# Transposing p of ten tiles with VectorE and transfers instead of TensorE

## The chip, the cores and the metric

The kernel runs on one core of one Trainium2 chip, in one launch. The metric is the device time of that launch in microseconds (us). The program is built once and run several times; the median is given.

The engines are called as in the profile: PE is TensorE (matmuls; PEld are its weight loads), DVE is VectorE, ACT is ScalarE, POOL is GpSimd, SP is SyncE, which here issues nearly all DMAs. Each engine works through its own list of instructions in order, and waits for others by semaphores.

## What is computed

Two layers, each a Fourier mixing and then a mixture of 256 experts (PEER), on 2048 tokens of width 512, all in float32:

```python
def layer(x):
    xn = layernorm(x)
    a, b = xn @ dft_hid_re.T, xn @ dft_hid_im.T         # 512 x 512
    x = x + dft_seq_re @ a - dft_seq_im @ b             # 2048 x 2048
    xn = layernorm(x)
    q = einsum("nd,dhc->nhc", xn, w_q)                  # 32 heads, 2 x 128
    s1, s2 = q[..., :128] @ k1.T, q[..., 128:] @ k2.T   # 16 scores each
    # per head: the best 2 of s1 and of s2, their 4 sums, the best 2 of these
    g = softmax(top_s)                                  # over those 2
    act = gelu(einsum("nd,nhkd->nhk", xn, u[top_e]))
    return x + einsum("nhk,nhk,nhkd->nd", g, act, v[top_e])
```

The kernel doesn't gather rows of u and v. It computes gelu(xn @ u.T) for all 256 experts, multiplies it by a 2048 x 256 matrix of gates (the sum over heads of g at the experts that were picked), and calls the product p. The layer's output is then x + p @ v. Float32 accuracy comes from splitting each operand in a high part, rounded to what the matmul takes in one pass (float32r), and the low rest: high x high, high x low and low x high are three matmuls that add up in one PSUM bank.

## The kernel before, in words

**Tiles and units.** The 2048 tokens are 16 tiles of 128. The product with the sequence matrices, "seq", goes in units: seven units of 256 tokens (two tiles each) and two of 128 (one tile each), `ORDER` says in which order, and `at` is a unit's place in it, 0 to 8. In layer 0 the order is as numbered, so `at` 2 to 6 are tiles 4 to 13. A unit's seq is 16 steps over the tokens s, each of four matmul groups of three (L518), on pieces of the sequence matrix that are streamed: L454 loads a piece `raw` (four buffers), L458 makes its high part `ch` on ACT, L462 its low part `cl` on DVE (three buffers each).

**A token tile** (`token_tile`, L610) follows when its unit's seq is done. PE multiplies by the hidden matrices (L668), DVE adds the rows of x (L682) and takes the layernorm's statistics, ACT writes xn (L705). xn is transposed, multiplied by the folded query weights (L784, L788) and by u (L818). DVE then picks the experts (L880 to L1009), and the gates of the tile are built by small matmuls (L1057), copied (L1089), stored in DRAM (`gdr`, L1116) and loaded back as `gt` (L1124), one buffer. L1131 multiplies `act` by `gt`: that is p, 128 tokens x 256 experts, in the buffer `act` (three of them).

For the product with v, p has to be transposed, experts on the partitions. Before the change that is done like this in layer 0: `f_pt` (L1162) transposes p's two halves of 128 x 128 on PE into a PSUM bank, ACT copies the high part into `pp` (L1167), DVE makes the low part (L1170), six matmuls multiply by v's parts (L1181, L1185), DVE adds the result to the row (L1218), and the row is stored as `x2d` (L1228), from where layer 1 loads it (L1243).

**Two ways without PE are in the kernel already.** xn of layer 0's units from `at` 2 on (and of most of layer 1) is transposed by `turned` (L716): DVE transposes the 16 x 4 blocks of 32 x 32 each in its place (L722), SP stores the tile in DRAM (`xdr`, L726), and four DMAs (L735) read it back, one for each 32 rows, with the blocks in their new places; ACT and DVE then make the parts (L742, L745). And in layer 1 `deferred` tiles have p's blocks turned by DVE (L1138), split (L1142, L1145) and stored (L1153); their product with v is made at the end (`off`, L566).

**What sets the order.** The order of every engine's instructions is written out ahead, by a planner (`Plan`, L78). Each step is an `op` with an engine, an estimated time, what it comes after, which buffers it takes (`take`) and which it is the last user of (`last`), a priority, and for DMAs `lag`, the time from issue to landing, and `shy`, an extra allowance. The planner plays this through and sorts the steps by their planned start; seq steps fill PE's time between the steps of tiles. On the chip each engine then keeps to that order, also where a step is late. A change of one step's engine or time lets all later steps be ordered anew.

Of the kernel before, what the change touches and what calls it, by code (L numbers as in the profile page):

```python
# [8 lines left out]
F32 = mybir.dt.float32  # L9
# [7 lines left out]
P = 128  # L17
# [21 lines left out]

def MOVED(layer, at):  # L40
    return at >= 2 if layer == 0 else at < NCH + NSC * (TPC - 1) - 2


def DEFERRED(layer, at):
    return layer == 1 and at < NCH + NSC * (TPC - 1) - 2
# [32 lines left out]
class Plan:  # L78
# [10 lines left out]
    def op(self, engine, us, fn, after=(), take=(), last=(), prio=(0, 0), lag=0.0, behind=(), shy=0.0):  # L89
        o = Op(len(self.ops), engine, us, fn, [a for a in after if a is not None], list(take), list(last), prio, lag,  # L90
               list(behind), shy)
        for h in o.last:
            h.users += 1
        self.ops.append(o)
        return o
# [63 lines left out]
def dve(n, rate=1):  # L159
    return 0.069 + n / (0.96e3 * rate)  # L160


def act(n):
    return 0.09 + n / 1.2e3
# [7 lines left out]
def spectral_peer_kernel(ctx: ExitStack, tc, x_in, cseq, ctile, dhid, wq, k1t, k2t, ut, vm, out):  # L172
# [7 lines left out]


    BUFS = {"acc": 4, "bank": 4, "raw": 4, "c": 3, "p": 1, "row": 4, "wr": 5, "wp": 2,
            "tok": 3, "sc": 1, "eq": 1, "act": 3, "q": 2, "top": 1, "qt": 1, "lr": 4, "gt": 1, "pp": 1, "gdr": 2, "xdr": 2, "bn": 1, "pick": 1}
    plan = Plan(BUFS)


# [41 lines left out]
    def work(shape, dtype, name, pool=None):  # L228
        return work_pool().tile(shape, dtype, name=name, bufs=BUFS[pool or name])

    def as32(ap):
        return ap.bitcast(F32)
# [377 lines left out]
    def token_tile(layer, n, i, t0, at):  # L610
# [2 lines left out]
        late = (0, layer, at, i, 1)  # L613
        fine = prio[:3] == FINAL
        moved = MOVED(layer, at)
        deferred = DEFERRED(layer, at)
        hrow = Hold("row")
        t = {}

# [490 lines left out]
        for hf in range(0 if fine else 2):  # L1110
            def f_out(hf=hf):
                if hf == 0:
                    t["gdr"] = dram.tile([2, E, 4, ROW], F32, name="gdr", bufs=BUFS["gdr"])
                d = t["gdr"][0]
                d = bass.AP(d.tensor, d.offset + hf * 8 * STEP, [[ROW, P], [STEP, 8], [1, 4 * E]])
                nc.sync.dma_start(d, t["gs", hf].rearrange("p g t e -> p g (t e)"))  # L1116
            moves.append(op("SP", 0.6, f_out, evac[hf:hf + 1], behind=moves[-1:], take=[] if hf else [hd], last=[hgs[hf]], prio=prio, lag=2.7))
        for j in range(0 if fine else 2):
            def f_in(j=j):
                if j == 0:  # L1120
                    t["gt"] = work([P, E, E], F32, "gt")
                d = t["gdr"][j]
                d = bass.AP(d.tensor, d.offset, [[STEP, 64], [4 * ROW, E], [1, E]])
                nc.sync.dma_start(t["gt"][j * 64:(j + 1) * 64], d)  # L1124
            back.append(op("SP", 0.6, f_in, moves, behind=back, take=[] if j else [hgt], last=[hd], prio=prio, lag=3.2, shy=0.5))
        if fine:
            a = op("PE", PICKS, f_picks, evac, take=[hgp], last=hgs[:1], prio=prio)
            a = op("DVE", dve(N), lambda: nc.vector.tensor_mul(t["act"].rearrange("p (e f) -> p e f", f=E), t["act"].rearrange("p (e f) -> p e f", f=E),
                                                               t["gp"].rearrange("p f e -> p e f")), [a, a_act], last=[hgp], prio=prio)
        else:  # L1130
            a = op("DVE", dve(N), lambda: nc.vector.tensor_mul(t["act"], t["act"], t["gt"].rearrange("p e f -> p (e f)")),  # L1131
                   back + [a_act], last=[] if deferred else [hgt], prio=prio)

        hb, hpp = Hold("bank"), Hold("c" if fine else "pp")

        if deferred:
            def f_turn():
                nc.vector.transpose(t["gt"].rearrange("p e f -> p (e f)"), t["act"])  # L1138
# [30 lines left out]
        def f_pl():  # L1169
            nc.vector.tensor_sub(t["pl"], t["pt"], as32(t["ph"]))  # L1170

        a = op("PE", 2 * TR32, f_pt, [a], take=[hb], last=[hact], prio=prio)
        a_ph = op("ACT", act(N), f_ph, [a], take=[hpp], prio=prio)
        a = op("DVE", dve(N), f_pl, [a_ph], last=[hb], prio=prio)
        hb = Hold("bank")

        def f_poh():
# [167 lines left out]
```

## Time and profile before

| | |
|---|---|
| time, median of 3 runs | 1233.59 us (1233.14 to 1234.08) |
| the profiled execution's own time | 1233.48 us |
| its span, first to last instruction | 1231.7 us |
| PE busy | 1220.1 us, 99% of the span |
| DVE busy | 1000.1 us, 81% |
| ACT busy | 492.2 us, 40% |
| DMA queue of SP: packets' time, share of 16 engines | 48.2% |
| transposes of p on PE (L1162) | 38, of which 20 are those of tiles 4 to 13 |

The page of the profile gives each engine's busy time. "Groups" are rows of instructions of one line, with the count, the busy time in us, the mean in ns, and the idle time of the engine just before them with what ended it. A "timeline" lists an engine's instructions by start time; `x2` means that two in a row were merged, and square brackets hold idle time before the instruction. Matmuls are pipelined: a matmul's duration overlaps the next one's, so that what one costs PE is read from the difference of start times.

### The profile page before, as it was taken

The page shows a single profiled execution, that of the slowest core. Times are in us where ns is not written, and L with a number is a line of the kernel's source. Part 1 is how long each engine was busy: PE and PEld are TensorE (multiplying, and loading weights), DVE is VectorE, ACT ScalarE, POOL GpSimd, SP SyncE. Part 2 cuts the span into 40 slices and gives each one's busy share as a digit, 9 for nine tenths or more (in the row PEclk, how much of TensorE's full clock was granted, in tenths as well). Part 3 has the DMA queues.
Part 4 walks back from the last instruction along what each step waited for, and adds up shares of the span by engine and source line. Part 5 has one row for each costly group of instructions (what it writes and reads, how often), then busy time and mean ns, then how long its engine had stood idle before and what let it go on. Part 6 is the DMA issues. An engine that isn't in the chain of part 4 may idle for free. (4 is left out here: it accounts for less than half of the span.)

```text
span 1231.7 us, 20733 instructions
## 1 busy us (share of the span) xinstructions
PE 1220.1 (99%) x7626; PEld 1014.5 (82%) x7626; DVE 1000.1 (81%) x2272; ACT 492.2 (40%) x1010; POOL 45.0 (4%) x71
## 2 busy tenths in 40 slices
PE   9999999999999999999999999999999999999998
PEld 6877778878788888899988988788888888888886
DVE  8899997999897785968987359959596786859796
ACT  7522234334343333324654233334343333343455
POOL 2000000000000000000000000000000000000000
PEclk9999999999999999999999999999999999999999
DMA  7866551453444244441656243563635254454464
GB/s 241 261 200 218 188 169 35 101 119 83 123 122 113 70 116 116 107 120 49 172 142 174 79 120 82 125 135 92 154 97 140 73 145 111 99 141 104 115 204 144
DMA packets 312726, 160.12 MB, mean 130 GB/s; under 512 B 216752, under 2 KB 283056, under 8 KB 312624
## 3 DMA queue, kind: packets, MB, share of 16 engines
q1 hardware_dynamic: 312480, 158.66, 48.2%
q8 instruction: 60, 0.98, 0.3%
q14 instruction: 42, 0.34, 0.1%
q10 hardware_dynamic: 144, 0.13, 0.0%
HBM read 120.73 MB, written 38.01 MB: 129 GB/s over the span
## 5 line engine op out<-in xcount | busy, mean ns | idle before, releaser
L518 PE MATMUL acc<-ch,xh 128*128 128x512 f32 (+1 forms) x868 | 328.3, 378 | 0.8 <-DVE ptl L547 0.8
L518 PE MATMUL acc<-cl,xh 128*128 128x512 f32 (+1 forms) x868 | 321.9, 371 | 0.0
L518 PE MATMUL acc<-ch,xl 128*128 128x512 f32 (+1 forms) x868 | 321.7, 371 | 0.0
L458 ACT CAST ch<-raw 128x512 fp32r<-128x512 f32 x256 | 158.6, 620 | 272.0 <-PE acc L518 222.7
L462 DVE TENSOR_TENSOR cl<-raw,ch 128x512 fp32r<-128x512 f32 x256 | 176.0, 688 | 61.6 <-ACT ch L458 51.4
L518 PEld LDWEIGHTS acc<-cl,xh 128*128 128x128 f32 x868 | 163.6, 188 | 28.8
L518 PEld LDWEIGHTS acc<-ch,xh 128*128 128x128 f32 x868 | 163.6, 189 | 28.0 <-issue 1.8
L518 PEld LDWEIGHTS acc<-ch,xl 128*128 128x128 f32 x868 | 163.8, 189 | 25.6
L880 DVE TENSOR_TENSOR tmp<-sc 128x512 f32<-128x512 f32 (+1 forms) x64 | 43.5, 680 | 72.9 <-ACT sc L793 72.6
L784 PE MATMUL bank<-wh,tok 128*128 128x512 f32 x256 | 100.3, 392 | 0.3 <-ACT tok L742 0.3
L784 PE MATMUL bank<-wl,tok 128*128 128x512 f32 x256 | 99.7, 389 | 0.0
L668 PE MATMUL bank<-dh,pth 128*128 128x512 f32 x248 | 98.6, 397 | 0.0
L668 PE MATMUL bank<-dl,pth 128*128 128x512 f32 x248 | 96.7, 390 | 0.0
L668 PE MATMUL bank<-dh,ptl 128*128 128x512 f32 x248 | 93.6, 390 | 0.0
L793 ACT COPY sc<-bank 128x512 f32<-128x512 f32 x62 | 36.1, 588 | 138.1 <-PE bank L788 108.0
L1041 DVE TENSOR_TENSOR lr<-iota,qt 128x1024 f16<-128x1024 f16 x124 | 81.0, 686 | 12.0 <-ACT qt L1022 11.9
L260 POOL TENSOR_TENSOR stats<-stats,half 128x1 f32<-128x1 f32 x64 | 43.7, 689 | 1149.1 <-DVE stats L257 1135.1
L867 DVE TENSOR_TENSOR eq<-sc,val 128x1024 f16<-128x1024 f32 (+1 forms) x64 | 77.2, 1207 | 1.5
L518 PE MATMUL acc<-ch,xg 128*128 128x512 f32 (+1 forms) x204 | 77.3, 379 | 0.0
L518 PE MATMUL acc<-cl,xg 128*128 128x512 f32 (+1 forms) x204 | 75.7, 371 | 0.0
L518 PE MATMUL acc<-ch,xm 128*128 128x512 f32 (+1 forms) x204 | 75.7, 371 | 0.0
L788 PE MATMUL bank<-wh,tok 128*128 128x512 f32 x256 | 68.4, 389 | 0.0
(190 smaller groups left out, 2057.8 us busy)
## 6 DMA issues: line engine op xcount, KB each, us to landing
raw<-in_cseq SPq DMA_DIRECT2D x224, 256.0 KB, 2.8
wr<-in_wq SPq DMA_DIRECT2D x32, 512.0 KB, 3.8
gdr<-lr SPq DMA_DIRECT2D x62, 256.0 KB, 3.7
raw<-in_ctile SPq DMA_DIRECT2D x32, 256.0 KB, 2.9
xdr<-lr SPq DMA_DIRECT2D x25, 256.0 KB, 2.8
tok<-xdr SPq DMA_DIRECT2D x100, 64.0 KB, 2.6
wr<-in_x SPq DMA_DIRECT2D x16, 256.0 KB, 3.3
row<-in_x SPq DMA_DIRECT2D x16, 256.0 KB, 4.0
```

The source lines that it names most:

```text
L260: nc.gpsimd.tensor_tensor(st[:, 1:2], st[:, 1:2], half, op=ALU.pow)
L458: nc.scalar.copy(t[1], t[0])
L462: nc.vector.tensor_sub(t[2], t[0], as32(t[1]))
L518: nc.tensor.matmul(target(d), w[s][:, d * P:(d + 1) * P], moving(s % per, part), start=(s == 0 and k == 0 and d % blocks == 0), stop=(s == ...
L668: nc.tensor.matmul(t["y", cs.start], w[:, k, c, t0:t0 + P], r[:, c, k, cs], start=(not fine and z == 0 and c == 0 and m == 0), stop=(z == ...
L784: nc.tensor.matmul(t["pc", hf], t["th"][:, k, :], r[:, k, hf], start=(k == 0 and r is wh), stop=False)
L788: nc.tensor.matmul(t["pc", hf], t["tl"][:, k, :], wh[:, k, hf], start=False, stop=(k == KD - 1))
L793: nc.scalar.copy(t["sc"][:, :, hf, :], t["pc", hf].rearrange("p h e -> p e h"))
L867: nc.vector.tensor_tensor(t["eq"][:, :, cols], scores(), val(rank_, cols), op=ALU.is_equal)
L880: nc.vector.tensor_max(t["tmp"][:, :, cols], flat("sc")[:, :8, cols], flat("sc")[:, 8:, cols])
L1041: nc.vector.tensor_tensor(t["m", hf, r], io2, row_of(r, hf), op=ALU.is_equal)
```

## The change

For the tiles of layer 0 at units 2 to 6 (ten tiles), the two transposes of p on PE are replaced. DVE transposes the 32 x 32 blocks of `act` into `gt`, each in its place. SP stores `gt` in a DRAM tile `pdr` (two buffers), 128 KB, each partition's 256 numbers as one run. Four DMAs read it back into `act`, 32 KB each, in runs of 32 numbers, with the blocks moved to their new places, so that `act` then holds p transposed. ACT copies the high part into `pp` and DVE makes the low part, now both from `act` in SBUF. The buffer `gt` is let go when its store has landed, `act` after the low part; the PSUM bank of `f_pt` isn't used in these tiles.

```diff
+def P_MOVED(layer, at):
+    return layer == 0 and 2 <= at < 7
...
-            "tok": 3, ..., "gdr": 2, "xdr": 2, "bn": 1, "pick": 1}
+            "tok": 3, ..., "gdr": 2, "xdr": 2, "pdr": 2, "bn": 1, "pick": 1}
...
-        deferred = DEFERRED(layer, at)
+        deferred, p_moved = DEFERRED(layer, at), P_MOVED(layer, at)
...
             a = op("DVE", dve(N), lambda: nc.vector.tensor_mul(t["act"], t["act"], t["gt"].rearrange("p e f -> p (e f)")),
-                   back + [a_act], last=[] if deferred else [hgt], prio=prio)
+                   back + [a_act], last=[] if deferred or p_moved else [hgt], prio=prio)
...
-        a = op("PE", 2 * TR32, f_pt, [a], take=[hb], last=[hact], prio=prio)
-        a_ph = op("ACT", act(N), f_ph, [a], take=[hpp], prio=prio)
-        a = op("DVE", dve(N), f_pl, [a_ph], last=[hb], prio=prio)
+        if p_moved:
+            hdp = Hold("pdr")
+
+            def f_turn():
+                nc.vector.transpose(t["gt"].rearrange("p e f -> p (e f)"), t["act"])
+
+            def f_out():
+                t["pdr"] = dram.tile([4, 32, 2, 4, 32], F32, name="pdr", bufs=BUFS["pdr"])
+                nc.sync.dma_start(t["pdr"].rearrange("i d k j t -> (i d) (k j t)"), t["gt"].rearrange("p e f -> p (e f)"))
+
+            a = op("DVE", dve(N), f_turn, [a], prio=prio)
+            b = op("SP", 0.35, f_out, [a], take=[hdp], last=[hgt], prio=prio, lag=2.3)
+            back = []
+            for j in range(4):
+                def f_in(j=j):
+                    nc.sync.dma_start(t["act"][32 * j:32 * j + 32].rearrange("p (k i t) -> p k i t", i=4, t=32),
+                                      t["pdr"][:, :, :, j, :].rearrange("i d k t -> d k i t"))
+                back.append(op("SP", 0.35, f_in, [b], behind=back[-1:], last=[hdp], prio=prio, lag=2.8, shy=1.0))
+
+            def f_ph():
+                t["pp"] = work([P, 2, N], F32R, "pp")
+                t["ph"], t["pl"] = (t["pp"][:, m].rearrange("p (k t) -> p k t", t=P) for m in range(2))
+                nc.scalar.copy(t["pp"][:, 0], t["act"])
+
+            def f_pl():
+                nc.vector.tensor_sub(t["pp"][:, 1], t["act"], as32(t["pp"][:, 0]))
+
+            a_ph = op("ACT", act(N) + 0.05, f_ph, back, take=[hpp], prio=prio)
+            a = op("DVE", dve(N), f_pl, [a_ph], last=[hact], prio=prio)
+        else:
+            a = op("PE", 2 * TR32, f_pt, [a], take=[hb], last=[hact], prio=prio)
+            a_ph = op("ACT", act(N), f_ph, [a], take=[hpp], prio=prio)
+            a = op("DVE", dve(N), f_pl, [a_ph], last=[hb], prio=prio)
```

More of the change, by code (lines that the diff above doesn't have):

```diff
@@ L182, in spectral_peer_kernel @@
     BUFS = {"acc": 4, "bank": 4, "raw": 4, "c": 3, "p": 1, "row": 4, "wr": 5, "wp": 2,
-            "tok": 3, "sc": 1, "eq": 1, "act": 3, "q": 2, "top": 1, "qt": 1, "lr": 4, "gt": 1, "pp": 1, "gdr": 2, "xdr": 2, "bn": 1, "pick": 1}
+            "tok": 3, "sc": 1, "eq": 1, "act": 3, "q": 2, "top": 1, "qt": 1, "lr": 4, "gt": 1, "pp": 1, "gdr": 2, "xdr": 2, "pdr": 2, "bn": 1, "pick": 1}
     plan = Plan(BUFS)
```

## The prediction

> **What bounds the kernel now.** I read the page first, then the busy time in the stretch in which the change lies, then the groups of that stretch, then the PE's timeline there. The page:
>
> ```profile
> span 1231.7 us, 20733 instructions
> PE 1220.1 (99%) x7626; PEld 1014.5 (82%) x7626; DVE 1000.1 (81%) x2272; ACT 492.2 (40%) x1010; POOL 45.0 (4%) x71
> PE acc L518 18%; PE bank L668 5%; PE bank L784 4%; PE bank L788 2%; PE acc L597 1%; PE bank L818 1%; PE bank L1057 1%; PE acc L668 0%; DVE eq L867 0%; DVE cl L462 0%; DVE tmp L880 0%; DVE tmp L887 0%; DVE eq L903 0%; DVE eq L897 0%; DVE lr L1041 0%
> ```
>
> The chain of waits runs over PE's matmuls. A busy PE need not be a full one, so the next question is whether PE's matmuls follow each other at their own pace where the change is made. That is 320 to 640 us: the windows' row, and the transposes' row of the groups in that stretch (x20 is ten tiles with two transposes each, so the count agrees with the change), the only other PE group there with idle time, and the transposes' start times.
>
> ```profile
> 320.00:640.00 320.00, 318.79 (x1917) 270.36 (x1916) 257.31 (x617) 128.41 (x263) 12.44 (x19) 1.00 0.44 112
> ...
> L1162 PE MATMUL bank<-identf,act 128*128 128x128 f32 x20 | 3.9, 275 | 0.9 <-DVE act L1131 0.9
> L784 PE MATMUL bank<-wh,tok 128*128 128x512 f32 x80 | 31.4, 392 | 0.3 <-ACT tok L742 0.3
> L1162 PEld LDWEIGHTS bank<-identf,act x20: 137/140/142, 322.7 to 621.7; 128*128 128x128 f32 x20
> ```
>
> PE is busy for 318.79 of 320 us, and has idle time before two groups only, 0.9 us before one of the transposes and 0.3 us before one L784. DVE is busy for 257.31 us, so it has 62.7 us over; the granted clock is 1.00. So here a matmul less is time less, and a wait more is time more.
>
> **What the removed transposes cost.** Their row's mean of 275 ns is a pipelined duration, not their share of PE. That is read from start times, in PE's timeline around one pair:
>
> ```profile
> 395.84 0.39 PE L518 MATMUL acc<-ch,xh 128*128 128x512 f32 x1
> 396.07 0.39 PE L518 MATMUL acc<-ch,xl 128*128 128x512 f32 x1
> 396.30 0.39 PE L518 MATMUL acc<-cl,xh 128*128 128x512 f32 x1
> 396.53 0.38 PE L1162 MATMUL bank<-identf,act 128*128 128x128 f32 x2
> 396.67 0.48 PE L518 MATMUL acc<-ch,xh 128*128 128x512 f32 x1
> 396.98 0.39 PE L518 MATMUL acc<-ch,xl 128*128 128x512 f32 x1
> ```
>
> L518 matmuls start every 0.23 us (395.84, 396.07, 396.30). From 396.30 to 396.98 lie two of their steps and the pair: 0.68 - 2 x 0.227 = 0.23 us for a pair. Ten pairs: **2.3 us**.
>
> The Trainium skill ("TensorE: Matmul & The Clock Gate", Part 4: PE-mode transpose) gives about 275 ns for a transpose within a kernel; the row's 275 ns agrees. Taken as PE time that would be 20 x 0.275 = 5.5 us, an estimate from that page; the start times say less than half, and they decide.
>
> **The wait that goes with them.** One of the ten pairs also waits, the first (tile 4):
>
> ```profile
> 321.44 0.39 PE L518 MATMUL acc<-cl,xh 128*128 128x512 f32 x1
> 322.70 0.44 PE L1162 MATMUL bank<-identf,act 128*128 128x128 f32 x2 [0.88 <-DVE act L1131]
> 322.89 0.47 PE L518 MATMUL acc<-ch,xh 128*128 128x512 f32 x1
> 323.21 0.39 PE L518 MATMUL acc<-ch,xl 128*128 128x512 f32 x1
> ...
> 321.63 0.69 DVE L462 TENSOR_TENSOR cl<-raw,ch 128x512 fp32r<-128x512 f32 x1
> 322.23 0.42 DVE L1131 TENSOR_TENSOR act<-act,gt 128x256 f32<-128x256 f32 x1
> ```
>
> From 321.44 to 323.21 are 1.77 us; less two steps (0.45) and the pair (0.23) that leaves a wait of 1.09 us. PE waited for DVE's L1131, which stood behind other work of DVE (L462 just before it). After the change PE has nothing that hangs directly on L1131: what is late next is the turn on DVE, then two DMAs, and only then the six matmuls L1181 and L1185. Bounds: 1.09 us gained (PE has sequence matmuls meanwhile) or nothing (DVE is still late for something else). I take 1.09, since the L518 that fill the place run on ch and cl pieces made ahead, in three buffers each.
>
> **What is added, and what covers it.** The nearest rows are the same steps that xn already takes in this layer (L722 turn, L726 out, L735 back, L742 and L745), and p's turn in layer 1:
>
> ```profile
> L1138 DVE STREAM_TRANSPOSE gt<-act 128x256 f32<-128x256 f32 x13 | 5.8, 443 | 0.1
> L1142 ACT CAST pp<-gt 128x256 fp32r<-128x256 f32 x13 | 5.3, 407 | 29.4 <-DVE gt L1138 29.4
> L1167 ACT CAST pp<-bank 128x256 fp32r<-128x256 f32 x18 | 6.8, 375 | 11.3 <-PE bank L1162 11.2
> L1145 DVE TENSOR_TENSOR pp<-gt,pp 128x256 fp32r<-128x256 f32 x13 | 5.5, 422 | 2.1 <-ACT pp L1142 2.1
> L1170 DVE TENSOR_TENSOR pp<-bank,pp 128x256 fp32r<-128x256 f32 x18 | 7.6, 422 | 4.6 <-ACT pp L1167 4.5
> L726 SPq DMA_DIRECT2D xdr<-lr x25: 319/332/817, 265.7 to 1085.4; - x25
> DMA to landing us min/median/max: 2.0/2.8/4.3
> ...
> L735 SPq DMA_DIRECT2D tok<-xdr x100: 562/628/845, 268.3 to 1101.6; - x100
> DMA to landing us min/median/max: 2.2/2.6/3.7
> ...
> SPq L454 <- DVE cl L462: 320.4, 129, 15.0
> SPq L735 <- DMA xdr<-lr: 6.0, 6, 1.6
> ```
>
> DVE: ten turns of 0.443 us are 4.4 us, within its 62.7 us; the subtraction costs 422 ns from either source. ACT: the copy costs 407 instead of 375 ns, 0.3 us in ten tiles, within 191.6 us of idle. SP: per tile one issue of 0.33 us and four of at most 0.63 us (L735's, which carry 64 KB where these carry 32 KB), 28 us in all; SP's raw loads L454 waited 320 us in all for raw buffers, so its queue has room. If that cover were gone, each issue would cost its own length in late raw loads. A return that waits on SP for the landing of the out transfer holds up the raw loads behind it: L735 did so 6 times, at most for 1.6 us. Raw has four buffers and ch three, and a piece feeds 12 matmuls, 2.7 us, so this reaches PE only after some pieces. Of DMA there is room too: its share in this stretch is 0.44.
>
> The path of one tile gets longer: 0.44 (turn) + 2.8 (out) + 3 x 0.63 (the issues of the first three back) + 2.6 (the last lands) + 0.41 + 0.42 = 8.6 us from the multiplication to L1181, with the shortest and longest of these rows 7.2 to 11.8 us; the multiplication now ends at 322.65 and L1181 starts at 324.37. So the six matmuls slide by some 7 us, over about 30 sequence matmuls, which the order written by the planner puts in their place. Three things are held that much longer: row and act, and gt until the out transfer has landed. Only one gt exists; the next tile's load:
>
> ```profile
> 344.63 1.33 SPq L1124 DMA_DIRECT2D gt<-gdr  x2
> ...
> 630.01 0.57 SPq L1228 DMA_DIRECT2D x2d<-row  x1
> ...
> 651.09 0.42 SPq L1243 DMA_DIRECT2D raw<-x2d  x1
> ```
>
> It comes 22 us after the multiplication at 322.65, and gt is free 0.44 + 2.8 (at most 4.3) us after it. Costed at nothing. At the end of the stretch the last moved tile's x2d store, at 630.0, slides to about 637, still ahead of the last reload at 651.1. If that cover of 14 us were gone, PE would wait for layer 1's xh by the difference.
>
> What is left is PE waiting for a p that returns later than planned. The nearest row is L784, which reads xn returned on the same way: one wait in this stretch, in PE's timeline and in the group of its copy on ACT,
>
> ```profile
> 601.36 0.28 PE L518 MATMUL acc<-cl,xg 128*128 128x256 f32 x1
> 601.97 0.50 PE L784 MATMUL bank<-wh,tok 128*128 128x512 f32 x1 [0.34 <-ACT tok L742]
> L742 ACT CAST tok<-tok 128x512 fp32r<-128x512 f32 x10 | 6.2, 618 | 2.9 <-DVE row L1218 2.7 <-DMA tok<-xdr 0.2
> ```
>
> of 0.61 less a step of 0.12 (a 128x256), 0.5 us in ten tiles. Bounds for ten p: none, and 1.09 us in each (tile 4's wait, the longest PE wait that the stretch shows), 10.9 us. I take 0.5, the row of the same transfers.
>
> **Sum**, against the profiled execution's own 1233.48 us (1231.7 of span and 1.8 around it; 0.1 below the median of 1233.59): 1233.5 - 2.3 - 1.1 + 0.5 = **1230.6 us**.
>
> **The rivals.**
> *The wait moves on.* DVE was behind at 321 us and gets a turn on top, so another instruction of PE catches the delay (L784 of the next tile needs L745, also on DVE). For it: L1131 started with no idle time of DVE before it. Against: DVE is busy for only 257 of 320 us. Then 1233.5 - 2.3 + 0.5 = 1231.7 us.
> *Later waits go as well.* The order of all engines is planned anew after tile 4. Two waits that have nothing to do with the change may fall away, the 0.5 us at 601 and this one:
>
> ```profile
> 791.24 0.40 PE L518 MATMUL acc<-cl,xh 128*128 128x512 f32 x1
> 792.46 0.47 PE L518 MATMUL acc<-ch,xh 128*128 128x512 f32 x1 [0.82 <-DVE ptl L547]
> ```
>
> of 1.22 - 0.23 = 1.0 us: 1230.6 - 1.5 = 1229.1 us. Nothing in the profile says that new ones don't come in their place.
> *Gain eaten up.* Waits of about 0.3 us in each of the ten tiles, by landings between the median and the longest, give the 3.4 us back: 1233.5 us.
> *The other side.* ACT and SP work in order, so a p that lands late holds up on ACT the ch copies behind it, and PE stands before L1181 with nothing else. Its price is up to 1.09 us a tile: 1233.5 - 3.4 + 10.9 = 1241.0 us. It decides from 0.34 us a tile (no gain) and makes the kernel slower by over 0.2% from 0.59 us. For it: landings spread from 2.2 to 3.7 us and 2.0 to 4.3 us. Against: xn takes this way with a copy on ACT too, and cost PE one wait in ten. The Trainium skill ("DMA: Bandwidth & Descriptors", Latency and other measured facts) puts HBM's access at 0.2 us on average and 2 us under high load, which would lengthen two landings at once; at a DMA share of 0.44 the landings above do not show it.
> *It doesn't do what it says.* Were PE not the bound, the transposes would go without any gain, 1233.6 us; the 318.79 of 320 us speak against it.
>
> **How the numbers follow.** About 0.2%, 2.5 us, is what a measurement of this kernel can tell from no change; so faster begins below 1231.1 and slower above 1236.1 us. Chances: the forecast 0.45 (1229.6 to 1231.6 by itself, since the 0.5 us may be nothing or double), the wait moves on 0.27, later waits go 0.11, gain eaten up 0.09, the other side 0.06, no effect 0.02. Faster: most of the first (0.38), all of the third, and 0.03 of the second, 0.52; slower 0.06; the same 0.42. The range reaches from a little beyond the third case to the fourth, 1228.8 to 1233.5 us; it leaves out the other side and the ends of the other cases.
>
> **What would show it.** Right: L1162 has 18 matmuls instead of 38; L518 starts every 0.23 us through tile 4's place, with no PE idle time by L1131; PE's busy time stays at 99% and the span is about 3 us shorter; L1181 follows the multiplication by 7 to 12 us. Wrong: PE idle time before L1181 or L784 in more than one or two tiles, ended by ACT's copy of p or by the return transfer; ch copies that wait for the returned act; DVE or SP at their limit in 320 to 640 us; a longer wait where layer 1 begins.

## The result and the profile after

The changed kernel takes 1235.61 us (median of 20 runs, 1234.76 to 1237.25) where the kernel before takes 1233.93 us beside it (20 runs): a ratio of 1.0016, 95% interval 1.0010 to 1.0022. It is slower by 1.2 to 2.7 us. The prediction was 1230.6 us, faster, with a range of 1228.8 to 1233.5 us; the time lies above it. The change is a small loss, under the 0.2% that the prediction took as the least clear difference, but the interval of the ratio does not reach 1.

Lines of the changed kernel from L458 on stand 4 later than before (L518 is L522, L1131 is L1135, L1162 is L1166); after L1174 come the new ones: L1180 the turn, L1184 the store, L1191 the returns, L1198 and L1201 the two parts of `pp`, L1215 and L1219 the product with v, L1277 the reload for layer 1. The page of the changed kernel begins:

```profile
span 1233.8 us, 20802 instructions
PE 1218.8 (99%) x7606; PEld 1012.0 (82%) x7606; DVE 1003.0 (81%) x2282; ACT 488.4 (40%) x1010; POOL 47.5 (4%) x71
```

PE has 20 instructions fewer and is busy for 1.3 us less, yet the span is 2.1 us longer: PE stands idle for more. Where, the busy times by stage say. Each row holds the stretch, its length, then busy time and count of PE, PEld, DVE, ACT and POOL, the granted clock, the DMA share and GB/s. First the kernel before:

```profile
225.00:320.00 95.00, 94.35 (x556) 76.76 (x555) 91.11 (x233) 36.90 (x84) 6.07 (x7) 1.00 0.45 106
320.00:400.00 80.00, 79.12 (x455) 64.36 (x454) 66.81 (x168) 30.19 (x65) 3.64 (x6) 1.00 0.47 117
480.00:560.00 80.00, 80.00 (x503) 69.43 (x502) 57.58 (x134) 28.52 (x59) 2.63 (x4) 1.00 0.40 100
560.00:640.00 80.00, 79.66 (x538) 70.59 (x538) 73.27 (x178) 41.69 (x83) 3.01 (x4) 1.00 0.48 126
640.00:760.00 120.00, 120.00 (x728) 103.31 (x727) 77.69 (x170) 48.23 (x92) 2.72 (x5) 1.00 0.43 117
```

and the changed kernel:

```profile
320.00:400.00 80.00, 78.65 (x446) 63.81 (x445) 67.88 (x171) 29.12 (x64) 4.92 (x6) 1.00 0.50 123
480.00:560.00 80.00, 80.00 (x504) 69.32 (x504) 60.13 (x139) 28.52 (x59) 2.16 (x4) 1.00 0.43 103
560.00:640.00 80.00, 78.47 (x526) 68.89 (x525) 73.03 (x181) 40.72 (x83) 5.71 (x5) 1.00 0.51 132
640.00:760.00 120.00, 118.34 (x719) 101.75 (x718) 76.72 (x167) 46.24 (x90) 2.71 (x5) 1.00 0.44 117
```

In the middle tiles PE is full in both. PE idle time grows in 560 to 760 us, from 0.34 to 3.19 us: there the last moved tiles, 12 and 13, meet the beginning of layer 1, whose reloads, the two parts xh and xl of its input, and first tiles' work are being made at the same time. The rows of before also show what the prediction averaged away: DVE's "62.7 us over" lie in the middle (58 of 80 us busy at 480 to 560); it is busy for 91 of 95 us ahead of tile 4 and for 73 of 80 us at 560 to 640.

The waits of PE in the changed kernel (who waited for whom: us in total, times, longest), from 320 to 595 us and from 595 to 705 us:

```profile
PE bank L1022 <- DVE q L1011: 0.9, 1, 0.9
PE bank L1219 <- DVE pp L1201: 0.3, 1, 0.3
PE acc L522 <- DVE ptl L551: 0.2, 1, 0.2
...
PE bank L1166 <- DVE act L1135: 1.1, 1, 1.1
PE bank L1215 <- ACT pp L1198: 0.8, 1, 0.8
PE bank L672 <- ACT pth L548: 0.6, 1, 0.6
PE bank L1022 <- DVE q L989: 0.5, 1, 0.5
```

Before, the second stretch has one wait, the 0.3 us of L784 that the prediction shows.

From here on a wait is counted as the prediction counted it: the time between two starts of PE's matmuls less the usual step (so L1135's 1.1 us count 1.30), and all those over 0.18 us in a stretch are added up. Three terms then make up the difference of 2.1 us:

| | before | after | difference |
|---|---|---|---|
| ten pairs of transposes | 2.3 | 0 | -2.3 |
| waits from 320 to 595 us | 1.04 | 1.05 + 0.47 + 0.32 = 1.84 | +0.8 |
| waits from 595 to 705 us | 0.50 | 0.28 + 0.96 + 0.78 + 1.30 + 0.68 = 4.00 | +3.5 |
| sum | | | +2.0 |

The wait of 1.0 us near 791 us is in both. So the question for the experiments: what made the 3.5 us where layer 1 begins, the round trips through DRAM, the turns on DVE, or the order in which the planner put everything anew?

The groups of the changed kernel's new steps and of what is left of the transposes (count, busy time, mean in ns, idle time before):

```profile
L1180 DVE STREAM_TRANSPOSE gt<-act 128x256 f32<-128x256 f32 x10 | 4.4, 441 | 0.1
L1201 DVE TENSOR_TENSOR pp<-act,pp 128x256 fp32r<-128x256 f32 x10 | 4.2, 422 | 12.5 <-ACT pp L1198 12.5
L1198 ACT CAST pp<-act 128x256 fp32r<-128x256 f32 x10 | 4.0, 405 | 2.5 <-DMA act<-pdr 2.5
L1166 PE MATMUL bank<-identf,act 128*128 128x128 f32 x18 | 3.6, 283 | 1.4 <-DVE act L1135 1.4
```

Its two transfers, with the shortest, median and longest issue in ns and the time from issue to landing:

```profile
L1184 SPq DMA_DIRECT2D pdr<-gt x10: 320/345/459, 323.5 to 620.2; - x10
DMA to landing us min/median/max: 1.7/2.1/4.9
...
L1191 SPq DMA_DIRECT2D act<-pdr x40: 562/607/1178, 328.4 to 624.9; - x40
DMA to landing us min/median/max: 2.0/2.2/3.2
```

And the one wait of SP's queue that is new, from 320 to 705 us:

```profile
SPq L1191 <- DMA pdr<-gt: 13.5, 8, 3.2
```

The single prices came out as taken: 441 ns for the turn, 405 and 422 ns for the parts, landings of about 2 us. With them L1215 starts 9.5 to 12.1 us after the multiplication ends, in each of the ten tiles; before it was 1.7 to 5.0 us, so the slide is 7 us on average, as forecast. Two things stand out. A return of 32 KB holds SP for 607 ns, nearly as long as xn's of 64 KB (628 ns); the planner was told 0.35 us. And the first return stood in SP's queue waiting for the store's landing in 8 of ten tiles, 13.5 us in all, where xn's did so 6 times in 25 for 6.0 us.

One of the waits, step by step in the changed kernel's timelines of SP, ACT and PE (start, duration, engine; in brackets the idle time before and what ended it):

```profile
596.01 0.37 SPq L1184 DMA_DIRECT2D pdr<-gt  x1
597.18 0.38 SPq L458 DMA_DIRECT2D raw<-in_cseq  x1
597.61 0.46 SPq L626 DMA_DIRECT2D row<-in_x  x1
599.36 3.10 SPq L1191 DMA_DIRECT2D act<-pdr  x4
602.55 0.55 SPq L1277 DMA_DIRECT2D raw<-x2d  x1
...
605.40 0.81 ACT L275 ACTIVATE raw<-raw,stats 128x512 f32<-128x512 f32 x1 [2.48 <-DMA raw<-x2d]
606.12 0.39 ACT L1198 CAST pp<-act 128x256 fp32r<-128x256 f32 x1
...
606.56 0.50 PE L1215 MATMUL bank<-vh,pp 128*128 128x512 f32 x1 [0.78 <-ACT pp L1198]
```

SP is held from 598.07 to 599.36 for the landing of the store, and to 602.46 by issuing four returns. Only then does it issue layer 1's reload. ACT stands 2.48 us for that reload, p's copy is next behind it in ACT's order, and PE's L1215 waits for the copy. The first of p's returns had been issued 6.8 us before its copy began.

### The profile page after: what moved, and what is told of

It reads as the page before. It is cut to its first block, busy times and chain, and to the rows that moved or that the text cites. A ratio compares the mean times of both kernels' runs of the same rounds, so it can differ in the third digit from the quotient of the medians.

```text
span 1233.8 us, 20802 instructions
## 1 busy us (share of the span) xinstructions
PE 1218.8 (99%) x7606; PEld 1012.0 (82%) x7606; DVE 1003.0 (81%) x2282; ACT 488.4 (40%) x1010; POOL 47.5 (4%) x71
## 5 line engine op out<-in xcount | busy, mean ns | idle before, releaser
L522 PE MATMUL acc<-ch,xh 128*128 128x512 f32 (+1 forms) x868 | 327.5, 377 | 1.0 <-DVE ptl L551 1.0
L522 PE MATMUL acc<-cl,xh 128*128 128x512 f32 (+1 forms) x868 | 321.7, 371 | 0.0
L522 PE MATMUL acc<-ch,xl 128*128 128x512 f32 (+1 forms) x868 | 321.7, 371 | 0.0
L522 PEld LDWEIGHTS acc<-ch,xh 128*128 128x128 f32 x868 | 163.7, 189 | 28.6 <-issue 2.3
L522 PEld LDWEIGHTS acc<-cl,xh 128*128 128x128 f32 x868 | 163.6, 188 | 28.5
L522 PEld LDWEIGHTS acc<-ch,xl 128*128 128x128 f32 x868 | 163.8, 189 | 25.6
L672 PE MATMUL bank<-dh,pth 128*128 128x512 f32 x248 | 98.4, 397 | 0.6 <-ACT pth L548 0.6
L672 PE MATMUL bank<-dl,pth 128*128 128x512 f32 x248 | 96.7, 390 | 0.0
L672 PE MATMUL bank<-dh,ptl 128*128 128x512 f32 x248 | 93.4, 390 | 0.0
L264 POOL TENSOR_TENSOR stats<-stats,half 128x1 f32<-128x1 f32 x64 | 46.2, 729 | 1148.4 <-DVE stats L261 1062.4
L522 PE MATMUL acc<-ch,xg 128*128 128x512 f32 (+1 forms) x204 | 77.2, 378 | 0.0
L522 PE MATMUL acc<-cl,xg 128*128 128x512 f32 (+1 forms) x204 | 75.7, 371 | 0.0
L522 PE MATMUL acc<-ch,xm 128*128 128x512 f32 (+1 forms) x204 | 75.6, 371 | 0.0
```

Of the source, the lines that this page charges most:

```text
L264: nc.gpsimd.tensor_tensor(st[:, 1:2], st[:, 1:2], half, op=ALU.pow)
L522: nc.tensor.matmul(target(d), w[s][:, d * P:(d + 1) * P], moving(s % per, part), start=(s == 0 and k == 0 and d % blocks == 0), stop=(s == ...
L672: nc.tensor.matmul(t["y", cs.start], w[:, k, c, t0:t0 + P], r[:, c, k, cs], start=(not fine and z == 0 and c == 0 and m == 0), stop=(z == ...
```

## Experiments

All were timed beside the kernel before. "Waits" are the sums in the two stretches, as in the table above.

### Which tiles carry the loss

Three kernels move fewer tiles:

```diff
-    return layer == 0 and 2 <= at < 7
+    return layer == 0 and 3 <= at < 6        # e1_mid: tiles 6 to 11
+    return layer == 0 and at == 2            # e2_first: tiles 4 and 5
+    return layer == 0 and at == 6            # e3_last: tiles 12 and 13
```

> The change on the six tiles 6 to 11 alone (units 3 to 5 of layer 0). Theory A, crowded places: the changed kernel loses its gain by PE waits at two places where DVE has little room, at tile 4 (320 to 335 us) and around tiles 12 to 14 (595 to 662 us, while layer 1's x is reloaded); the six tiles between cost no wait and give 0.23 us each: 1.4 us less than the kernel before, ratio 0.9989, and PE in 340 to 590 us without waits of over 0.3 us. Theory B, any new order: what the planner puts elsewhere falls anywhere, so waits of several us turn up also here, after the last changed tile: 0 to 4 us more than before. Theory C, every tile pays: the loss of 1.7 us on ten tiles is 0.17 us a tile, here 1.0 us more than before.

> The change on tiles 4 and 5 alone (unit 2). Theory A: two pairs (0.46 us) and tile 4's wait of 1.09 us go, and the waits that the changed kernel shows at 327 us (1.05), 334 us (0.47) and 383 us (0.32) come: 0.3 us more than before, ratio 1.0002, and nothing new after 400 us. Theory C: 0.35 us more. Theory B: waits of 1 us and over after 400 us that neither kernel has.

> The change on tiles 12 and 13 alone (unit 6). Theory A: nearly all of the loss is here. Two pairs (0.46 us) go, the waits at 597 (0.28), 605 (0.96), 614 (0.78), 655 (1.30) and 662 us (0.68) come, the one of 0.5 at 601 goes: 3.0 us more than before, ratio 1.0025. Theory C: 0.35 us more, ratio 1.0003. Theory B: anything, with waits also after 700 us.

| | ratio | median (before 1233.87) | waits 320-595 | waits 595-705 |
|---|---|---|---|---|
| tiles 6 to 11 | 0.9998 [0.9990, 1.0007] | 1234.00 | 1.40 | 0.79 |
| tiles 4, 5 | 0.9991 [0.9983, 1.0000] | 1233.15 | 1.47 | 0 |
| tiles 12, 13 | 1.0031 [1.0020, 1.0042] | 1237.97 | 1.00 | 4.42 |

The last two tiles alone lose as much as the full change and more: 4.42 us of waits stand where layer 1 begins, for a saving of 0.46 us. They are not the same waits, though: the largest are at 603 (1.77) and 693 us (1.42), so the order there is another one. Tiles 6 to 11 alone gave no gain in time, where 0.9989 was expected without waits. In the profile PE ends 0.7 us earlier: a new wait of 0.39 us at 457 us and 0.3 us more of waits where layer 1 begins stand against the 1.4 us. In the middle, PE's sequence matmuls come earlier tile by tile: in the full change the same one of their number starts 0.05 us earlier than before at 365 us and 1.15 us earlier at 546 us. With the new wait of 0.32 us at 383 us, which lies between, the six pairs gave 1.10 + 0.32 = 1.42 us, 0.24 us each. That is the forecast price of 0.23 us a pair. (Tiles 6 to 11 alone give 1.47 us between the same places, counted in the same way.)

### What in the round trip costs

Three kernels change one part each of the full change: the turn does an eighth of its columns, the returns bring one block of 32 x 32 each, or POOL issues the returns (here the planner wrote a new order).

```diff
-  nc.vector.transpose(t["gt"].rearrange("p e f -> p (e f)"), t["act"])
+  nc.vector.transpose(t["gt"].rearrange("p e f -> p (e f)")[:, :32], t["act"][:, :32])   # e4_short_turn
...
-  nc.sync.dma_start(t["act"][32 * j:32 * j + 32].rearrange("p (k i t) -> p k i t", i=4, t=32),
-                    t["pdr"][:, :, :, j, :].rearrange("i d k t -> d k i t"))
+  nc.sync.dma_start(t["act"][32 * j:32 * j + 32, :32], t["pdr"][0, :, 0, j, :])          # e5_small_back
...
-  back.append(op("SP", 0.35, f_in, ...
+  back.append(op("POOL", 1.0, f_in, ...                    # e10_pool_back, with nc.gpsimd.dma_start
```

> The changed kernel with all ten tiles in the same order of all engines, but DVE turns only the first 32 of p's 256 columns, so p of these tiles is not transposed and the output is not the reference's; a turn takes some 0.1 instead of 0.44 us, everything else stays. If DVE's own extra work is what makes it late: the waits at 327, 334, 605, 614, 655 and 662 us (5.3 us in all) shrink by a third to a half, 2 to 3 us less than the changed kernel, near 1233 us, ratio to before 0.999 to 1.000. If the transfers are (SP's queue that stands before the return, ACT's that stands before its copy): within 0.5 us of the changed kernel, ratio 1.001 to 1.002.

> The changed kernel with all ten tiles, same order of all engines, but each of the four return transfers brings only 32 x 32 numbers (one block) instead of eight blocks for its 32 rows, so p of these tiles is mostly not transposed and the output is not the reference's. Theory S, SP's queue: a return holds SP for 0.61 us (the planner reckons 0.35), forty of them; the reloads of x behind them land late, ACT's copies and DVE's subtractions stand behind these, and PE behind those. If the small returns hold SP for 0.35 us only, the waits at 597 to 662 us (4.0 us) shrink to under half: 2 us less than the changed kernel, ratio to before about 1.000. Theory O, the order itself: at the layer change there is no slack, and the order that the planner makes there loses whatever the transfers take: ratio 1.001 to 1.002 like the changed kernel.

> The changed kernel with the four return transfers of p issued by POOL instead of SP (POOL is busy for 4% of the span), so SP issues only p's store, ten more DMAs instead of fifty. The planner orders the engines anew with that. Theory S: the reloads are not held up, the waits at 597 to 662 us go or shrink below 1.5 us in sum, and the gain of the transposes shows: ratio 0.998 to 0.999. Theory O: the order is another one, the waits at the layer change stay at 3 to 6 us: ratio 1.000 to 1.003.

| | ratio | waits 320-595 | waits 595-705 |
|---|---|---|---|
| full change | 1.0016 [1.0010, 1.0022] | 1.84 | 4.00 |
| short turn | 1.0013 [1.0003, 1.0022] | 1.47 | 5.04 |
| one block back | 1.0005 [0.9996, 1.0014] | 1.39 | 2.55 |
| returns by POOL | 1.0044 [1.0032, 1.0057] | 1.36 | 7.14 |

DVE's turn is not the cause: with an eighth of it left the time is the same. Its waits from 595 to 705 us even sum to 1.0 us more, in the same order and with less work. Each sum comes from one profiled execution, so differences of about 1 us between two of them prove little.

The returns have a part. With one block each, in the same order of work, they are issued in 414 instead of 607 ns (median):

```profile
L1191 SPq DMA_DIRECT2D act<-pdr x40: 324/414/1277, 328.9 to 623.2; - x40
```

The waits at 334, 597 and 605 us are gone, the last being the one shown step by step, and the ratio falls from 1.0016 to 1.0005, by 1.4 us. 2.55 us of waits stay. Taking the returns off SP's queue did not help: it was worse than either expectation. But its order is another one, so it does not tell the two apart.

Two more told the planner other numbers: `shy=3.0` instead of 1.0 for the returns (e6_allow3), and 0.65 us for each issue of a return, xn's too (e9_sp_cost).

> The changed kernel with all ten tiles, the planner told that p's return may land 2 us later than it reckoned (3.0 instead of 1.0 us of allowance). If a return that is late against the plan is the cause (PE before L1215, ACT and SP in order behind it): the waits for p's copy at 334 and 605 us (1.4 us) go, 1 to 2 us less than the changed kernel, ratio 1.000 to 1.0008. Theory O: just another order, with 3 us and more of waits at the layer change: ratio 1.001 to 1.003.

> The changed kernel with the planner told that a return transfer holds SP for 0.65 us, for p's and for xn's (it reckoned 0.35 and 0.3), the landing at the same time as before in sum. Theory S: SP's work at the layer change is spread as the chip does it, the waits there fall to about half: ratio 0.999 to 1.0005. Theory O: a new order, with waits of 3 to 6 us at the layer change: ratio 1.001 to 1.003.

More allowance gave 1.0003 [0.9994, 1.0012], with 1.29 + 1.17 + 0.37 us of waits from 595 to 705 us. The truer issue time gave 1.0100 [1.0085, 1.0116], most of it at the very end of layer 1, 7.4 us. Both ask for a better plan and get a different one; in e9_sp_cost the plan is worse where nothing of the change is.

### Orders without any transfer

Can an order by itself cost as much? Three kernels are the kernel before, p on PE, with another number in the planner: `WARY`, an allowance for PE, at 0.7 and 0.9 instead of 0.8, and p's low part of tiles 12 and 13 told to come 7 us later than it does. A fourth is the change for tiles 4 to 11 only, so that nothing is moved where layer 1 begins.

```diff
-WARY = 0.8
+WARY = 0.7        # e7_wary07;  0.9 in e8_wary09
...
-  a = op("DVE", dve(N), f_pl, [a_ph], last=[hb], prio=prio)
+  a = op("DVE", dve(N), f_pl, [a_ph], last=[hb], prio=prio, shy=7.0 if layer == 0 and at == 6 else 0.0)   # e11_late_order
...
-    return layer == 0 and 2 <= at < 7
+    return layer == 0 and 2 <= at < 6        # e12_4to11, in the changed kernel
```

> The kernel before, without the change, with one constant of the planner altered: the extra time that PE's steps keep from results of other engines, 0.7 instead of 0.8 us. No instruction is added or taken away, only the order differs. Theory O: waits of PE at the layer change and elsewhere come and go by 1 us and more: ratio off 1 by 0.1% or more, either way. Theory S: within 0.05% of before.

> The kernel before, without the change, with the same constant of the planner altered the other way: PE's steps keep 0.9 instead of 0.8 us from results of other engines. Theory O: order alone moves the time by 0.1% or more either way, as 0.7 did (1.0012). Theory S: within 0.05% of before, and the 0.7 was an exception.

> The kernel before, with no transfer of p at all: for tiles 12 and 13 alone the planner is told that p's low part is ready 7 us later than it is, so that it puts the six matmuls of these tiles and what follows as late as the change does; the instructions are the same. Theory O, order: the loss at the layer change comes from where the late p is put among reloads and the next unit, not from the transfers: PE waits of 2 to 4 us between 595 and 700 us, ratio 1.0015 to 1.003. Theory S, transfers and their queue: without them no waits, ratio 0.9995 to 1.0005.

> The change on the eight tiles 4 to 11 (units 2 to 5), none at the layer change. Eight pairs give 1.8 us and tile 4's wait 1.1 us; the waits at 327, 334 and 383 us (1.9 us) come. If the loss belongs to tiles 12 and 13: 1.0 us less than before, ratio 0.9992 (range 0.998 to 1.000), faster than both kernels. If any new order at the layer change loses, though its own tiles are unchanged: waits of 2 us and more between 595 and 700 us, ratio 1.000 to 1.002.

| | ratio | waits 595-705 |
|---|---|---|
| before | 1 | 0.50 |
| WARY 0.7 | 1.0012 [1.0003, 1.0020] | 2.30 |
| WARY 0.9 | 1.0005 [0.9996, 1.0014] | 2.21 |
| p of tiles 12, 13 planned late | 1.0045 [1.0032, 1.0058] | 5.08 |
| tiles 4 to 11 by blocks | 1.0036 [1.0022, 1.0050] | 6.69 |

It can: in these four, 2 to 7 us of waits stand from 595 to 705 us with no round trip there at all, and two of them lose more time than was expected of the order. It need not: tiles 4 and 5 alone and tiles 6 to 11 alone were planned anew as well, with no moved tile there, and have 0 and 0.79 us. PE's waits there in e12_4to11:

```profile
PE bank L1166 <- DVE act L1135: 1.4, 1, 1.4
PE bank L1022 <- DVE q L989: 1.1, 1, 1.1
PE bank L1061 <- DVE lr L1051: 0.8, 1, 0.8
PE bank L1022 <- DVE q L1011: 0.6, 1, 0.6
PE acc L522 <- ACT xg L290: 0.5, 1, 0.5
PE acc L522 <- DVE xm L291: 0.3, 1, 0.3
```

None of them is on p's way by blocks. At this point the order looked like the main cause.

### The order of before kept

Then the order itself was held: the plan is made as before, with p on PE, and only afterwards are the moved tiles' transposes taken out, the turn, the store and four returns put in by time, and the steps behind them (copy, low part, product, row and what follows) set later by some 9 us. The returns land in `pp`'s low half, so that `act` is free after the turn.

```diff
+    for w in swaps:                                  # after the plan is made
+        turn = extra("DVE", 0.44, w["turn"], [w["mul"]], pt.start)
+        put = extra("SP", 0.35, w["out"], [turn], turn.start + 0.6)
+        got = [extra("SP", 0.62, ..., [put], put.start + 3.2 + 0.62 * j) for j in range(4)]
+        least = got[-1].start + 3.4 - late[0].start
...
+            for o, was in zip(late, kept_starts):
+                o.start = was + least + 0.1 * step
```

> All ten tiles by the change's way, but the order of every engine is planned as if p were still transposed on PE; then, for each of the ten tiles, the two transposes are taken out, and the turn, the store and the four returns are put in at their earliest place, and p's parts, the six matmuls, the row's addition, its statistics and its store are moved some 9 us later, all else staying in the order of the kernel before. (The returns land in the low half of pp instead of act, as xn's do, since three buffers of act are not enough in that order.) Theory O, order: without a new order the waits of 4.0 us at 595 to 705 us do not come, and what is left is the gain of ten pairs, 2.3 us, and tile 4's wait, 1.0 us, less about 0.5 us for p that returns late: 1231.2 to 1232, ratio 0.9975 to 0.9985, faster than both kernels. Theory S, transfers: the forty returns do their harm in any order, ratio 1.000 to 1.002 with waits of over 2 us at the layer change.

> The same with the old order kept, for the eight tiles 4 to 11 alone (the set that cost 1.0036 when the planner was free to order anew). Theory O: eight pairs, 1.8 us, and 1.0 us of tile 4's wait less about 0.3: ratio 0.998 to 0.9988. Theory S: with no moved tile at the layer change no harm there, but then the 1.0036 of the same tiles in the free order stays unexplained.

> Tiles 6 to 11 alone go by blocks, and every instruction of before keeps its place in the order; the new ones are put in between, and what reads a returned block is set later by about 9 us. Theory (the price of 0.23 us a pair is right where DVE has room, and what is lost comes from the order at the crowded places): six pairs give 1.4 us, tile 4's wait of 1.04 us at 321 stays, nothing is added from 595 to 705 us, where no tile is moved: 1232.4 to 1232.9, ratio 0.9985 to 0.9992. Rival (the round trips cost by themselves wherever they are): waits of PE between 395 and 590 us that eat most of the 1.4 us, ratio 0.9995 to 1.001.

| by blocks, order kept | ratio | median (before) | waits 320-595 | waits 595-705 |
|---|---|---|---|---|
| tiles 4 to 13 (e13_kept_order) | 1.0060 [1.0047, 1.0072] | 1241.66 (1234.03) | 1.73 and a lower clock | about 7 |
| tiles 4 to 11 (e14_kept_4to11) | 1.0005 [0.9996, 1.0014] | 1234.92 (1234.03) | 2.76 | 0 |
| tiles 6 to 11 (e15_kept_6to11) | 0.9994 [0.9985, 1.0003] | 1232.82 (1233.86) | 1.44 | 0.34 |

With the order kept and no tile moved there, the beginning of layer 1 costs nothing (0, and 0.34 us). But with tiles 12 and 13 moved it costs about 7 us, in an order that is otherwise before's. So the new order was not the whole cause either. Tiles 4 to 11 missed the gain that was expected (0.998 to 0.9988): waits of 1.2 us at 339 us and 1.6 us at 355 us, near tiles 4 and 5, stand against it. The six middle tiles alone are the one place where the price comes out nearly clean; their waits from 320 to 705 us:

```profile
PE bank L1167 <- DVE act L1136: 0.8, 1, 0.8
PE bank L1216 <- ACT pp L1194: 0.3, 1, 0.3
PE bank L673 <- ACT pth L548: 0.2, 1, 0.2
```

Tile 4's old wait stays (1.0 us by starts), one p is late (0.43), and PE ends 1.3 us earlier than before. Up to 546 us, ahead of that late p, 1.55 us had been gained since 365 us, 0.26 us a pair. The median is 1.0 us lower, but the interval of the ratio includes 1, so it is not shown that this kernel beats the one before.

### The two orders without the round trips

Last, the same orders with the trips left out. In the first, the order is exactly the changed kernel's; turn, store and returns are empty, and `pp` is made from `act` as it stands. In the second, the order is that of e13_kept_order; the turn stays, store and returns are empty, and `pp` is made from `gt`.

```diff
             def f_out():
+                return
...
                 def f_in(j=j):
+                    return
...
             def f_turn():
-                nc.vector.transpose(t["gt"].rearrange("p e f -> p (e f)"), t["act"])
+                pass                                 # e16_order_alone only
```

> The changed kernel with the order of its engines as it is, but in the ten tiles the turn, the store and the four returns are left out: ACT and DVE make pp from act as it stands after the multiplication, so p goes into the product with v untransposed and the output is another. PE's work is that of the changed kernel. Order theory (the changed kernel's 4.0 us of waits from 595 to 705 us come mainly from where the planner put the steps): 2.5 us of them or more stay, and the time is 1234 us or above. Transfer theory (they come from ACT, DVE and SP being held up by late returns): at most 1 us of them stays, tile 4's 0.5 us at 334 goes, and the time is 1231 to 1232 us.

> The kernel with before's order kept and all ten tiles by blocks (the one that took 1241.7 us), with the store and the returns left out: DVE's turn stays, ACT and DVE make pp from gt, at the same late places of the order, so p's blocks are turned but not moved and the output is another. Transfer theory: the waits of 1.7 us at 338 us and of 7 us from 595 to 705 us go, and the time falls to 1231 to 1232 us. Order theory (it is the late places that cost): most of them stay, and the time is 1237 us or above.

| | ratio | median (before 1234.68) | waits 320-595 | waits 595-705 |
|---|---|---|---|---|
| the change's order, no trips (e16_order_alone) | 0.9982 [0.9973, 0.9991] | 1232.18 | 1.22 | 1.48 |
| kept order, no trips (e17_kept_no_trip) | 1.0035 [1.0022, 1.0049] | 1239.15 | 2.51 | 4.10 |

The waits of PE in e16_order_alone from 320 to 705 us:

```profile
PE bank L1022 <- DVE q L1011: 0.7, 1, 0.7
PE bank L1166 <- DVE act L1135: 0.6, 1, 0.6
PE bank L1022 <- DVE q L989: 0.5, 1, 0.5
PE acc L522 <- DVE ptl L551: 0.2, 1, 0.2
```

Against the changed kernel's list, the waits that end with p's own steps (L1201, L1198) are gone, so is L672's, and L1135's is about half as long. So the round trips are the main cause, against the theory of the order: in the same order without them the kernel is clearly faster than before, and by the ratios (1.0016 against 0.9982) they cost 4.2 us. Its 1232.18 us and 1.48 us of waits come close to what the theory of the transfers expected (1231 to 1232 us, at most 1 us). (The profiled execution took 1.7 us more than the median; the excess lies behind the last matmul, which ends 1.2 us earlier than before.) The waits show 3.1 us of that: 0.6 from 320 to 595 us and 2.5 (4.00 against 1.48) where layer 1 begins. Of the 3.5 us that this place lost, 1.0 us is left for the order (1.48 against 0.50). That 1.0 us is not clear of noise: by its ratio the run without trips is 2.2 us below the kernel before, 1.1 to 3.3 by the interval, which would also fit the full saving of 2.3 us and an order that costs nothing.

The one-block run stands between them, in the same order. By the waits, 1.1 us of the 2.5 stay with small returns (2.55 against 1.48; turn, store and four short issues) and 1.4 us come with their full size.

In the kept order the medians put 3.2 us on the trips (7.6 us above before with them, 4.5 us without; in the profiled execution part of the difference is a lower clock, below). The 4.5 us are the late places themselves: most of the waits stay without any trip, and 1239.15 us is what the theory of the late places expected. Its profiled execution was the fastest of its five, 2.6 us below the median, so the 2.51 and 4.10 us of waits in the table understate the usual run.

## Why the prediction was wrong

**What bounds the kernel: right.** PE is busy for 99% before and after, and every wait added shows up at the end: the three terms give +2.0 us, measured +2.1 us of span.

**Ten pairs for 2.3 us: right.** The group has 18 matmuls left of 38, and the saving comes out of PE's start times in the middle tiles wherever no wait hides it: 1.42 us for six pairs in the full change, 1.55 us in e15_kept_6to11. No kernel that computes the whole shows it clearly as time. The 275 ns of the row, taken as PE time, would have given more than twice as much.

**Tile 4's wait gone, 1.1 us: wrong.** It moved on, as the first rival had it: DVE is still late, and PE now waits 1.05 us for L1011 at 327 us, on the same engine. The turn, which the rival blamed, is not needed for it: without turn and trips 0.90 us of this wait stay, and the waits from 320 to 595 us are 1.22 us where they were 1.04. The prediction set DVE's 62.7 us over in 320 to 640 us against this; the row that decides is the one just ahead, 91.11 of 95 us busy. That is an average used for a place.

**One late return in ten, 0.5 us: the step that failed.** It was sized by what xn's returns cost in the same stretch. By the waits of PE the round trips cost 3.1 us: 0.6 near tile 4 (1.84 against 1.22) and 2.5 where layer 1 begins. The size is not spread over ten tiles; it is four waits in tiles 12 and 13 and their neighbours, and one in tile 4. The rival "the other side" had the mechanism, a late step that holds up ACT and SP behind it, but priced it for each tile alike. The view of SP shows the route: the first return waits for the store's landing in 8 of ten tiles, four issues take 3.1 us, and the reload behind them is late; that route is shown for one wait, and with short issues this wait is gone. The prediction named that route ("a return that waits on SP for the landing of the out transfer holds up the raw loads behind it") and looked only at raw pieces of the sequence matrix, which have several buffers in hand. It did not look at what else SP carries where layer 1 begins, although it had quoted a reload. Of the 4.9 us between the three terms of the forecast (-2.9 us) and the three measured ones (+2.0 us), 2.6 us are this step, 1.2 us tile 4's wait and 1.0 us the order.

**SP's queue has room: true of the sum, false of the place.** A return's issue of 0.61 us was bounded well by L735's 0.63. What cost was its place in the queue, ahead of a reload.

**Act, row, gt and x2d held longer, at nothing: not shown wrong.** The profile puts no wait of PE down to one of them coming free late.

**The order written anew, at nothing: by the waits of one execution wrong by 1.0 us** where layer 1 begins, by the times not shown. The prediction had it as a rival with a gain ("later waits go as well") and noted that nothing says that new ones don't come. The 0.5 us at 601 did go; 0.80 and 0.69 us came at 653 and 659 us. The six runs that were planned anew without any transfer there had 0, 0.79, 2.2, 2.3, 5.1 and 6.7 us of waits. So the order before, with 0.50 us, was a good one among these, and a new one lost more often than it won at that place. The 1.0 us near 791 us stayed in five of the six and is gone with `WARY` at 0.7, where another of 1.1 us stands at 1174 us.

**The signs of being wrong that it named** were seen in part: longer waits where layer 1 begins, and PE idle before L1215 and L1219 (its L1181 and L1185), ended by the copy and the low part of p. These are two tiles; the sign asked for more than one or two. PE at 99%, 18 transposes and L1215 7 to 12 us behind the multiplication, named as signs of being right, were seen as well and say nothing of the time.

What stays open: how the 1.1 us with small returns divide between the store's landing, the four issues and the turn was not measured; the 1.1 us of round trips between the ratios (4.2) and the waits (3.1) lie within the noise; and whether another order would take ten tiles without loss was only tried with the few above. The best by the middle of its interval that computes the whole is tiles 4 and 5 alone, 0.9991 [0.9983, 1.0000], and no run that computes the whole is clearly faster than before.

## What to carry to other kernels

Where one engine is full and the others have room on average, price a step at the place where it stands: take the busy rows of each stage, and in the crowded ones ask of every transfer which load stands behind it in its queue and which copy behind that. When an order is planned anew, the new order can have a price of its own; measure it by leaving the new work out and keeping the order. A saving of 0.23 us a step is soon lost to one wait of 1 us: even the six middle tiles, where the stage had room, were not shown to be faster.

## What was not expected of the hardware

**The clock fell to half after two short waits of one kernel.** In e13_kept_order PE waits 1.55 us by the profile at 338 us. Some 1.2 us after it its L522 matmuls start 0.43 instead of 0.23 us apart, for about 3 us, and the granted clock (the third column from the right in the busy times by stretch) falls to about a half. The kernel's timeline of PE there:

```profile
341.01 0.39 PE L522 MATMUL acc<-cl,xh 128*128 128x512 f32 x1
341.24 0.50 PE L522 MATMUL acc<-ch,xh 128*128 128x512 f32 x1
341.54 0.63 PE L522 MATMUL acc<-ch,xl 128*128 128x512 f32 x1
341.97 0.63 PE L522 MATMUL acc<-cl,xh 128*128 128x512 f32 x1
```

and its busy times by stretch:

```profile
338.60:340.00 1.40, 0.00 (x0) 0.00 (x0) 1.40 (x4) 0.00 (x0) 0.00 (x0) 1.00 0.58 94
340.00:341.25 1.25, 1.18 (x20) 1.01 (x21) 1.25 (x7) 0.40 (x1) 0.69 (x1) 1.00 0.53 83
341.25:343.75 2.50, 2.50 (x8) 1.92 (x7) 2.06 (x5) 1.41 (x4) 0.77 (x1) 0.53 0.37 79
```

That adds 1.4 us (seven steps of 0.2) to a wait that is 1.73 us by start times. After a second wait, 1.40 us by the profile (1.56 by start times) near 603 us, six such steps follow as well. Waits of the same length and longer did not do it elsewhere: 1.41 us at 354 us in e14_kept_4to11 and 2.20 us at 600 us in e10_pool_back were followed by a clock of 1.00, in the latter with matmuls 0.23 us apart:

```profile
602.00:603.50 1.50, 1.47 (x6) 1.23 (x7) 1.49 (x3) 0.50 (x1) 1.03 (x2) 1.00 0.90 268
```

So the length of the wait alone does not decide; what does was not found. The Trainium skill ("TensorE: Matmul & The Clock Gate", Part 1: What's actually happening) says that the clock falls to half after an idle window of about 3.4 us that runs on its own. The half is what the row shows (0.53), but here the fall came behind waits of 1.40 and 1.55 us, less than half of that.

**The issue of a strided return does not follow its size.** By the medians 32 KB hold SP for 607 ns, 64 KB for 628 ns; one block of 32 x 32, 4 KB, for 414 ns.
